# Batch 1 of a two-stage kernel: maxima and exponentials ahead of small sums, sums of the next batch at another place, left sums for two pairs in one instruction

## The chip, the cores and the metric

The kernel runs on one core of a Trainium2 chip. The metric is the device time of one execution in microseconds (us). The engines named below are TensorE (PE, with its weight loads as PEld), VectorE (DVE), ScalarE (ACT) and SyncE (SP), which issues the DMA transfers. Each engine works through its own list of instructions in order; they meet only where one waits for what another has written or read.

## The reference

An attention between tokens `x` and a small state, both ways, then a feed-forward block with the quick gelu. All is fp32. Cut to what matters:

```python
B, H, S, Ns, D = (8, 8, 512, 32, 64)      # d_model 512, d_ff 2048

scores = scale * x @ state^T               # softmax over the 32 states
xread = softmax(scores) @ state            # (B, H, 512, 64)
scores2 = scale * state @ x^T              # softmax over the 512 tokens
sread = softmax(scores2) @ x               # (B, H, 32, 64)
t = concatenate([xread, sread], axis=2)    # to (B*544, 512) for the next block
h = t @ w_in                               # (.., 2048)
g = h * (1.0 / (1.0 + np.exp(-1.702 * h)))
return g @ w_out                           # (.., 512)
```

## The kernel before

The kernel writes both products of the feed-forward block by a Strassen-Winograd scheme: 7 products of half the size instead of 8, at the price of sums of the matrices. For `w_out`, cut into quarters `B11`, `B12`, `B21`, `B22`, these are T1 to T4. For the second ("down") product most of the seven are split once more in the same way, so that each of B11, B21, B22, T1 to T4 has three small sums of its own (`low_sums`), and a third one in place (`low_third`). They are made once and kept in DRAM (`low_keep`, `low_away`), and loaded again for each batch.

```python
def low_sums(t, rooms):
    b11, b12, b21, b22 = halves_of(t)
    t1, t2, t4 = rooms
    return [(T_of, v) for v in ((t1, b12, b11), (t2, b22, t1), (t4, b21, t2))]   # DVE, L1281

def low_made(k, t, i):                 # sums made in the on-chip room low_a or low_b, and kept
    ...
def low_away(k, t):                    # sums made in a room of the tag "xT", and kept in DRAM
    room = apool.tile([P, NPR, S], FP32, tag="xT", name=f"away_{k}")...
```

The tag "xT" has one buffer. The exponentials of the scores over the tokens, `e2`, go into it too, and leave it by four DMAs (`squares<-e`):

```python
def att_s_exp(b, room=None):
    if room is None:
        room = e2_room[b] = apool.tile([P, NPR, S], FP32, tag="xT", name=f"e2_{b}")
    ...
        nc.scalar.activation(out=out, in_=src, func=AF.Exp, bias=a["mx2"][g], scale=scale, accum_out=sm)   # ACT, L386
```

A product of the small kind is seven groups of matmuls into three banks x, y, z (cut):

```python
def strassen_low(left, right, bank, R, at):
    product(x, a11, b11, True); nc.scalar.copy(y, x)      # L701
    at(1)
    product(z, s1, t1, True);   nc.scalar.copy(c22, z)    # L704
    at(2)
    product(y, s2, t2);         nc.scalar.copy(c12, y)    # L707
    at(3)
    product(x, a12, b21);       nc.scalar.copy(c11, x)    # L710
    at(4)
    product(y, a21, t3);        add(c22, y, c22)          # DVE, L697
    at(5)
    product(z, s4, b22);        add(c12, z, c12)          # DVE, L697
    at(6)
    product(y, a22, t4);        nc.scalar.copy(c21, y)    # L719
    at(7)
```

`at(i)` runs what is hooked at the place `P5.i`, `P6.i` and so on. Batch 1's down product has the order P1 (whole), P2 (whole; its halves have the hooks `P2a`, `P2b`), then P5, P6, P3, P7, P4 as small ones. In between stands the attention of batch 2: at `P2a` its scores, their transposes (`att_blocks`) and maxima (`att_s_max`), at `P2b` the exponentials.

```python
# P2, batch 1
product(bank(1), A_of(0, 1), B21, "P2")
tt(osb, bank(1), k1)               # DVE, L748: frees the bank that P5's second small product uses
```

The down product of batch 0 is done in eight pairs of blocks instead, because `w_out` is still arriving and being rounded at that time. Each pair `i` has four sums of the left matrix and four of the right one, on DVE, as instructions of 128 x 256:

```python
def pair_sums(i):
    ...
    steps = [
        (s1, a21, a22, ALU.add), (T1[:, f], B12[:, f], B11[:, f]), (s2, s1, a11), (t2, B22[:, f], T1[:, f]),
        (a21, a11, a21), (t4, B21[:, f], t2), (s4, a12, s2), (B12[:, f], B22[:, f], B12[:, f]),
    ]
    for v in steps if i else steps[::2] + steps[1::2]:
        tt(*v)                     # L1308
```

## Time and profile before

| | before |
|---|---|
| time, median of three runs | 703.92 us (703.5 to 704.36) |
| span of the profiled execution | 699.9 us |
| granted TensorE clock | 1.00 |
| PE idle from 160 to 175 us (15 us) | 2.89 us |
| PE idle from 175 to 187 us | 0.39 us |
| PE idle from 187 to 203 us | 0.00 us |
| PE idle from 203 to 230 us | 1.14 us |
| DVE busy from 187 to 203 us (16 us) | 15.86 us |

The rows of a stretch come from the table of busy time by stretches: its length less what the engine was busy. In it, 145 to 203 us is the down product of batch 1 with the attention of batch 2 beside it, and 203 to 230 us is batch 2's up product and the beginning of its down product. A releaser (the `<-`) is what ended an engine's wait. "PEld" is the weight load ahead of a matmul; it runs beside the matmul before.

### The profile page before, as it was taken

The page shows a single profiled execution, that of the slowest core. Times are in us where ns is not written, and L with a number is a line of the kernel's source. Part 1 is how long each engine was busy: PE and PEld are TensorE (multiplying, and loading weights), DVE is VectorE, ACT ScalarE, POOL GpSimd, SP SyncE. Part 2 cuts the span into 40 slices and gives each one's busy share as a digit, 9 for nine tenths or more (in the row PEclk, how much of TensorE's full clock was granted, in tenths as well). Part 3 has the DMA queues.
Part 4 walks back from the last instruction along what each step waited for, and adds up shares of the span by engine and source line. Part 5 has one row for each costly group of instructions (what it writes and reads, how often), then busy time and mean ns, then how long its engine had stood idle before and what let it go on. Part 6 is the DMA issues. An engine that isn't in the chain of part 4 may idle for free.

```text
span 699.9 us, 13779 instructions
## 1 busy us (share of the span) xinstructions
PE 683.3 (98%) x5357; PEld 578.5 (83%) x5359; DVE 571.7 (82%) x1226; ACT 320.7 (46%) x704; POOL 0.8 (0%) x8
## 2 busy tenths in 40 slices
PE   8989999998999999999999999999999999999996
PEld 3433587776898799889988999889988998999995
DVE  6999998998869989697969886988778895887540
ACT  5688843223336523654355434653376236422420
POOL 0000000000000000000000000000000000000000
PEclk9999999999999999999999999999999999999999
DMA  8921337056423474436551674157433740251001
GB/s 233 364 75 58 122 121 178 7 195 203 158 73 86 150 242 138 80 84 214 156 110 31 178 219 115 21 138 234 139 54 106 239 140 16 73 153 52 11 2 30
DMA packets 106321, 87.41 MB, mean 125 GB/s; under 512 B 64784, under 2 KB 85776, under 8 KB 106256
## 3 DMA queue, kind: packets, MB, share of 16 engines
q1 hardware_dynamic: 106256, 86.53, 42.5%
q8 instruction: 43, 0.70, 0.4%
q14 instruction: 22, 0.18, 0.1%
HBM read 68.94 MB, written 17.56 MB: 124 GB/s over the span
## 4 chain that ended last, share of the span: by engine, by line
PE 88%; DVE 5%; ACT 4%; DMA 2%; issue 1%; SPq 0%; DVEq 0%; ACTq 0%
PE low L692 27%; PE o L692 14%; PE o L1111 13%; PE upx L1111 5%; PE h L547 4%; PE o L1354 4%; PE M L329 4%; PE down L1354 3%; PE o L589 2%; PE upw L1111 2%; PE down_up L547 2%; PE o L741 1%; PE o L329 1%; PE warm L127 1%; PE upx_sr L1111 1%; DMA out_dram<-osb_sr 1%
## 5 line engine op out<-in xcount | busy, mean ns | idle before, releaser
L692 PE MATMUL low<-w_out,g 128*128 128x128 f32 x416 | 54.3, 276 | 0.0
L692 PEld LDWEIGHTS low<-w_out,g 128*128 128x128 f32 x416 | 50.5, 192 | 4.5 <-issue 3.4
L1111 PE MATMUL o<-ta,M 128*128 128x256 f32 x192 | 49.9, 382 | 0.0
L1111 PE MATMUL upx<-aT,M 128*128 128x256 f32 x192 | 49.3, 379 | 0.0
L692 PE MATMUL low<-low,g 128*128 128x128 f32 x336 | 43.5, 276 | 0.4 <-DVE later L697 0.4
L692 PEld LDWEIGHTS low<-low,g 128*128 128x128 f32 x336 | 40.3, 192 | 0.7 <-DVE later L697 0.6
L1111 PEld LDWEIGHTS o<-ta,M 128*128 128x128 f32 x192 | 35.5, 190 | 6.0 <-ACT g L1157 1.6
L1111 PEld LDWEIGHTS upx<-aT,M 128*128 128x128 f32 x192 | 36.0, 190 | 4.7
L476 ACT COPY M<-M 128x512 f32<-128x512 f32 x59 | 30.7, 594 | 16.9 <-PE M L329 16.9
L1117 ACT ACTIVATE g<-o 128x512 f32<-128x512 f32 (+1 forms) x56 | 31.4, 560 | 10.2 <-PE o L1111 10.2
L692 PE MATMUL low<-sums,later 128*128 128x128 f32 x280 | 35.8, 275 | 0.0
L692 PEld LDWEIGHTS low<-sums,later 128*128 128x128 f32 x280 | 33.6, 192 | 0.1
L329 PE MATMUL M<-w_in,stT 64*32 64x512 f32 x472 | 32.3, 595 | 0.4 <-ACT sr L524 0.4
L1111 PE MATMUL o<-ta,ms 128*128 128x256 f32 x120 | 30.8, 379 | 0.0
L547 PE MATMUL h<-aT,M 128*128 128x512 f32 x64 | 28.7, 599 | 1.4 <-ACT M L476 1.4
L1117 ACT ACTIVATE g<-g 128x512 f32<-128x512 f32 (+1 forms) x28 | 16.8, 600 | 23.4 <-DVE g L1120 23.4
L547 PEld LDWEIGHTS h<-aT,M 128*128 128x128 f32 x64 | 11.8, 190 | 18.3 <-issue 12.0
L1157 ACT COPY g<-o 128x512 f32<-128x512 f32 (+1 forms) x28 | 15.5, 555 | 24.4 <-PE o L1111 24.4
L227 ACT ACTIVATE low<-low,edge 128x512 f32<-128x512 int32 x30 | 21.5, 717 | 9.3 <-DVE low L216 9.2
L1111 PEld LDWEIGHTS o<-ta,ms 128*128 128x128 f32 x120 | 22.8, 190 | 3.1
L1111 PE MATMUL o<-aT,m 128*128 128x256 f32 x96 | 24.6, 379 | 0.0
L692 PEld LDWEIGHTS o<-w_out,g 128*128 128x128 f32 x160 | 19.4, 192 | 5.0 <-issue 5.0
(290 smaller groups left out, 1650.8 us busy)
## 6 DMA issues: line engine op xcount, KB each, us to landing
low<-low SPq DMA_DIRECT2D x108, 256.0 KB, 3.4
low<-low SPq DMA_DIRECT2D x11, 768.0 KB, 4.4
later<-in_moe_w_out_dram SPq DMA_DIRECT2D x16, 512.0 KB, 3.5
w_out<-in_moe_w_in_dram SPq DMA_DIRECT2D x12, 512.0 KB, 5.6
xsq<-in_x_dram SPq DMA_DIRECT2D x96, 64.0 KB, 2.4
xn<-in_x_dram SPq DMA_DIRECT2D x12, 512.0 KB, 4.5
out_dram<-osb SPq DMA_DIRECT2D x15, 256.0 KB, 2.2
out_dram<-later SPq DMA_DIRECT2D x14, 256.0 KB, 2.1
```

Of the source, the lines that this page charges most:

```text
L127: nc.tensor.matmul(ps, zeros[:, :P], zeros, start=True, stop=True)
L227: nc.scalar.activation(out=sc.bitcast(FP32), in_=sc, func=AF.Relu, bias=edge[0], scale=-8.0)
L329: nc.tensor.matmul(ps[g][st], A[b]["stT"][rows, st], rhs(rows, j), start=True, stop=True)
L476: nc.scalar.copy(m[:, g], ps[g])
L547: nc.tensor.matmul(hps, lhs[i], rhs[i], start=(i == 0), stop=(i == n - 1))
L589: nc.tensor.matmul(ps[:, r], lhs[f][:, P * r : P * (r + 1)], rhs[:, f], start=(first and r == 0 and f == 0), stop=(f == HF - 1), skip_grou ...
L692: nc.tensor.matmul(ps, lhs[f], rhs[:, f], start=(first and f == 0), stop=(f == QF - 1), skip_group_check=True)
L741: nc.tensor.matmul(ps[:, r], lhs[f][:, P * r : P * (r + 1)], rhs[:, f], start=(r == 0 and f == 0), stop=(f == HF - 1), skip_group_check=True,)
L1111: nc.tensor.matmul(ps[:, k], lhs[i][:, o : o + P], rhs[i], start=(first and k == 0 and i == 0), stop=(i == n - 1), skip_group_check=True,)
L1117: nc.scalar.activation(out=dst, in_=src, func=AF.Gelu_apprx_sigmoid)
L1157: nc.scalar.copy(c12, Y(u))
L1354: nc.tensor.matmul(ps7[name][:, HN * r : HN * (r + 1)], lhs[:, P * r : P * (r + 1)], rhs, start=(i == 0 and r == 0), stop=(i == HF - 1), s ...
```

## The change

Four things are moved; no matmul is added or taken away, and DVE has 16 instructions less.

- Pairs of batch 0: the left sums of two pairs are made in one instruction each (128 x 512 in place of twice 128 x 256), in rooms with four places; in the first pair the transposes of the exponentials stand between products P1 and P2, and batch 1's exponentials are made and scaled ahead of batch 0's.
- Batch 1, P2: T4's sums leave the place ahead of the maxima; the exponentials come at `P2a`, directly behind the maxima, ahead of T2's sums. T4's sums are made in P5 and P6, and the third sums of T3 and T4 a little later than before.
- B11's sums, which stood in batch 2's up product, are made ahead of it; B21's, which were spread over it and over the first small product, are made at once at its first free place.
- For this the helpers `left_sums`, `turns_of`, `T4_sum` and the rooms `s_rooms` are new.

It is meant to let the instructions that others wait for come ahead of the sums that nobody waits for yet.

```diff
-        at(p3, att_s_exp, b)
+        at("P2a" if first else p3, att_s_exp, b)
...
         if b == 2:
-            m0, m1 = (low_sums(t, r) for t, r in ((B11, low_b), (B21, low_a)))
             t0, t1, t2, t3 = ((turn_x, (b + 1, i)) for i in range(NPR))
-            more = [
-                [*m0, (low_keep, (0, turn_rooms[1]))],
-                [(low_third, (B11,)), t0],
-                [t1, t2, m1[0]],
-                [t3, m1[1]],
-            ]
-            for i, v in enumerate(more):
+            for i, v in enumerate([[], [t0], [t1, t2], [t3]]):
...
-    att_s_exp(0, room[:, :NG])
-    att_s_exp(1, room[:, NG:])
+    for b in (1, 0):
+        att_s_exp(b, room[:, NG * b : NG * (b + 1)])
     rounds(3)
-    att_s_norm(0)
-    att_s_norm(1)
+    for b in (1, 0):
+        att_s_norm(b)
...
+    def left_sums(i):
+
+        u = ORDER[i] // 2
+        (a11, a21), (a12, a22) = quarters(0, u, S), quarters(0, HF // 2 + u, S)
+        s1, s2, s4 = (v[:, i % 4 : i % 4 + 2] for v in s_rooms)
+        return [(tt, v) for v in ((s1, a21, a22, ALU.add), (s2, s1, a11), (a21, a11, a21), (s4, a12, s2))]
...
+        left = left_sums(i) if i % 2 == 0 else []
+        if i == 0:
+            first = left[:3]
+            turns_of(first)
+            turns_of(steps[:1] + left[3:] + steps[1:])
+        else:
+            turns_of([v for k in range(4) for v in left[k : k + 1] + steps[k : k + 1]])
...
         if i == 0:
-            pair(i, "P1", "P2")
+            pair(i, "P1")
             for b in (1, 0):
                 for g in range(NG):
                     att_eT(b, g, b == 1)
+            pair(i, "P2")
...
+    def T4_sum(i):
+
+        if i == 0:
+            away4.append(away(4))
+        fn, args = low_sums(T4, low_parts(away4[0]))[i]
+        fn(*args)
+        if i == 2:
+            low_keep(4, away4[0])
+
     for b in range(1, B):
+        if b == 2:
+
+            turns_of(low_sums(B11, low_b))
+            low_keep(0, turn_rooms[1])
+            low_third(B11)
         if b > 1:
-            ahead = {"P1.1": [(up_strassen(b, S, *parts_x(b), A[b]["sums"]), ())]}
-            if b == 2:
-                ahead["P1.5"] = [low_sums(B21, low_a)[2], (low_keep, (1, turn_rooms[0]))]
-                ahead["P1.6"] = [(low_third, (B21,))]
+            beside = [(turns_of, ([*low_sums(B21, low_a), (low_keep, (1, turn_rooms[0])), (low_third, (B21,))],))]
+            ahead = {"P1.1": [(up_strassen(b, S, *parts_x(b), A[b]["sums"], beside if b == 2 else ()), ())]}
         else:
             ahead = {
-                "P2a": [(low_away, (4, T4))],
                 "P2b": [(low_made, (2, T2, 0)), (low_third, (T2,))],
+                "P5.4": [(T4_sum, (0,))],
+                "P5.6": [(T4_sum, (1,))],
+                "P6.2": [(T4_sum, (2,))],
                 "P6.4": [(low_third, (B22,))],
-                "P3.1": [(low_third, (T3,))],
-                "P3.2": [(low_third, (T4,))],
+                "P3.4": [(low_third, (T3,))],
+                "P7.3": [(low_third, (T4,))],
             }
```

## The prediction

> **What bounds the kernel now.** I read four views, from coarse to fine. The first is the first part of the page, to see which engine fills the span.

> ```profile
> span 699.9 us, 13779 instructions
> ...
> PE 683.3 (98%) x5357; PEld 578.5 (83%) x5359; DVE 571.7 (82%) x1226; ACT 320.7 (46%) x704; POOL 0.8 (0%) x8
> ```

> TensorE (PE) is busy for 683.3 of 699.9 us. The change neither adds nor removes a matmul, so its whole possible gain is inside the 16.6 us in which PE stood still, and most of those lie in the start and the end that it doesn't touch. The second view, who waited for whom with PE alone, names the still time that it can touch (columns: waiting group, releaser, us in total, times, longest).

> ```profile
> PE o L692 <- DVE osb L748: 2.0, 1, 2.0
> ...
> PE low L692 <- DVE spare_M L748: 1.1, 1, 1.1
> ...
> PE low L692 <- ACT low L701: 0.9, 1, 0.9
> ...
> PE M L329 <- ACT sr L524: 0.4, 1, 0.4
> PE low L692 <- DVE later L697: 0.4, 1, 0.4
> PE o L1354 <- ACT sums L550: 0.3, 1, 0.3
> ```

> Together 5.1 us. The third view, the instructions in order of time from 145 to 174 us, shows what is behind the first and third of these (columns: start, us, engine, line, operation, idle time before).

> ```profile
> 160.15 2.05 ACT L476 COPY M<-M 128x512 f32<-128x512 f32 x4 [4.80 <-PE M L329]
> 160.85 3.32 PEld L741 LDWEIGHTS o<-w_out,g 128*128 128x128 f32 x16 [0.84 <-issue]
> ...
> 161.28 1.31 DVE L360 STREAM_TRANSPOSE e<-o 128x512 f32<-128x512 f32 x2
> 161.38 0.34 SPq L652 DMA_DIRECT2D low<-away  x1
> ...
> 165.80 1.28 ACT L386 ACT_TABLE_LOAD   x1 [3.59 <-DMA low<-away]
> ...
> 166.70 0.68 DVE L748 TENSOR_TENSOR osb<-o,g 128x512 f32<-128x512 f32 x1
> ...
> 167.44 1.16 PE L692 MATMUL o<-low,spare_M 128*128 128x128 f32 x8 [1.98 <-DVE osb L748]
> ...
> 169.13 0.33 ACT L701 COPY low<-low 128x128 f32<-128x128 f32 x1
> ...
> 169.32 2.71 SPq L484 DMA_DIRECT2D squares<-e  x4
> ...
> 169.51 1.16 PE L692 MATMUL low<-low,spare_M 128*128 128x128 f32 x8 [0.92 <-ACT low L701]
> ```

> There are two chains. VectorE (DVE) makes T4's sums from 159.15 to 161.28, then transposes and maxima, then T2's sums, and only at 166.70 the addition `osb` that frees a bank: PE stands still for 1.98 us. ScalarE (ACT) is done with its copies at 162.2, but the exponentials go into the buffer that T4's sums used, and wait 3.59 us until those have left it by DMA; the small copy L701 stands behind them: 0.92 us. The fourth view, the same from 196 to 240 us, shows the third wait, the 1.1 us in batch 2's first product: a sum of B21 stands directly ahead of the sum PE needs.

> ```profile
> 228.34 0.65 DVE L1281 TENSOR_TENSOR low<-w_out,low 128x512 f32<-128x512 f32 x1
> 228.91 0.75 DVE L748 TENSOR_TENSOR spare_M<-g,g 128x256 f32<-128x256 f32 x2
> ...
> 229.47 1.13 PE L692 MATMUL low<-low,spare_M 128*128 128x128 f32 x8 [1.15 <-DVE spare_M L748]
> ```

> [...]I count only idle time with a named releaser. [...]the trace shows 1.28 us and the exponential directly behind it (165.80 to 167.09), so I charge 1.28. [...](256 KB to the output land in 2.1 to 2.2 us).

> **Part 1, pairs.** Left sums for two pairs at once: 32 instructions of 256 become 16 of 512. In the trace a 256 starts about 0.34 us after the last, a 512 0.60: 2 x 0.34 - 0.60 = 0.08, times 16 = 1.3 us of DVE. But from 91 to 145 us PE is busy 54.00 of 54.00, so I count nothing. Ahead of it, the transposes eT now come before product P2. Both need the same gelu (it frees the first transpose's bank), so P2 cannot start before 79.2 and neither can the transposes; what moves is the four copies of eT on ACT, from 80.83 to the end of the gelus at 80.63: **0.2 us**, passed on through the wait of M L329.

> **Part 2, batch 1's maxima and exponentials ahead of T2 and T4.** DVE starts the transposes of the scores when the scores are done, about 159.25, not 161.28. Up to `osb` it then has the same work as before, 166.70 - 161.28 = 5.42 us, so `osb` starts at 164.67 and ends at 165.35. The product that waits for it could start, by the matmuls alone, about 165.3; weight load included I take 165.4, against 167.44. On ACT: copies end 162.2, table load to 163.5, the exponentials (2.2 us, 167.09 to 169.29) to 165.65, L701 to 165.95; the third product starts at 166.3, not 169.51. So far 3.2 us gained.

> **Part 3, where T4's sums went.** They now stand behind the fourth and sixth small product of P5 and the second of P6, in the same buffer as the exponentials. The first must therefore wait until the exponentials have left by the four DMAs squares<-e. These can be issued at 165.7; four issues took 2.71 us, so until 168.4, and then the last must land: 2.2 us after it was issued at 167.7 (the output's 2.1 to 2.2) is 169.9, and the queue is busy with x and with T2's sums until then, so I estimate 170.5. DVE reaches that sum at 164.67 + 7 operations of 0.60 = 168.9, and stands until 170.5, then 0.6 for the sum. Directly behind it is the addition L697 that the seventh product of P5 waits for; PE would come to that product at 169.9. Addition until 171.4: **PE stands about 1.4 us where it did not before.** From 3.2 that leaves 1.8.

> Further on T4's remaining two sums (0.6 each) fit in 1.57 and 1.50 us in which DVE waited for PE before. The third sums of T3 and T4 leave the stretch around 182.8 and 184.7: the addition L697 that PE waited for 0.39 us (186.24) is then early: gain 2.2. T4's third comes back in P7, where DVE is busy 15.86 of 16.00 us (187 to 203) and has no room: give back about 0.5. **Part 2 and 3: 1.7 us.**

> **Part 4, B11 and B21.** B11's four operations (2.65 us) now stand ahead of batch 2's up products, where DVE waited 3.14 us for ACT: free. B21's four follow the first addition and push the next by 0.4 us, which has slack. At the end the sum at 228.34 is gone; DVE's chain behind the addition at 224.59 (five operations, about 3.7 us) still ends at 228.3, so the wait of 1.15 shrinks by **0.6 us**, not wholly.

> **Sum:** 0.2 + 1.7 + 0.6 = 2.5 us; 703.92 - 2.5 = 701.4 us.

> **Rivals.** (a) The DMA is early: all waits go. If squares<-e has landed by 168.9, part 3's stall is nil and DVE keeps its lead: 3.2 + 0.4 + 0.6 + 0.2 = 4.4, so about 699.5. For it: without T4's 768 KB the queue has less ahead of these DMAs. Against: issue and landing alone reach 169.9. (b) A new wait takes the place of the old. The DMA lands at 172 or later, the stall is 3 us, and DVE, with no slack from 187 to 203, carries the loss on: gain 0 to 0.8, about 703.5. For it: before, the queue moved nothing much until about 1.7 us after the first issue (169.32 to 171). (c) DVE is the bound of batch 1's second product: what leaves one place on DVE only comes back in another, as it does the same work but for 1.3 us. Its idle time from 160 to 187 is 27 - 23.4 = 3.6 us, which is enough for a gain of some 2 but not of 4: about 702. (d) Nothing in the pairs: if the first pair's double-width sums delay product P6 there, 0.3 us is lost; T2's sum for it is done about when it was before (85.5), so I give this little.

> **Range and chances.** Rivals (a) and (b) span 699.5 to 703.5; the runs before spread by 0.9 us. Range 699.4 to 703.3. 2% is 14 us, nearly three times all the waits concerned: within 2% 0.985, faster 0.01, slower 0.005.

> **What would show it.** Right: DVE's `osb` starts directly after T2's sums and no wait for it over 0.2 us is left on PE; the table load follows the copies near 162.2; DVE waits 1 to 2 us for the DMA squares<-e ahead of the first T4 sum, and PE as long, less its lead, for L697; the wait at batch 2's first product is about 0.5. Wrong: no wait of DVE for squares<-e (rival a), or one above 2.5 us (b); or PE waits in P7 and P4 that sum to over 1 us (c); or any loss in 91 to 145 us.

## The result and the profile after

| | before | after |
|---|---|---|
| time, median | 704.01 us (703.5 to 704.36, 4 runs) | 700.44 us (699.63 to 701.43, 4 runs) |
| ratio, 95% interval | | 0.9951 (0.9933 to 0.9968) |
| span of the profiled execution | 699.9 us | 699.1 us |

The change gains 3.57 us, within 2%; 701.4 had been predicted. The profiled execution shows only 0.8 us of it, and that is the first riddle. The first part of the page of after:

```profile
span 699.1 us, 13774 instructions
...
PE 684.5 (98%) x5359; PEld 579.6 (83%) x5359; DVE 571.5 (82%) x1210; ACT 321.0 (46%) x704; POOL 0.8 (0%) x8
```

DVE has its 16 instructions less (1210 for 1226) and the same busy time. PE does the same matmuls and is busy 1.2 us longer: some of them were slower (the record of a small matmul takes 421 ns at 174 us, 275 at 178). Who waited for whom, PE alone, in after:

```profile
PE low L692 <- DVE spare_M L697: 1.9, 1, 1.9
...
PE o L692 <- DVE osb L748: 0.6, 1, 0.6
PE eT L504 <- ACT sums L550: 0.3, 1, 0.3
...
PE low L692 <- DVE later L697: 0.2, 1, 0.2
```

Of the six waits before, 5.1 us together, those for `osb` (2.0), the exponentials' L701 (0.9), batch 2's `spare_M` (1.1) and `sr` (0.4) are gone or down to 0.6; one new wait of 1.9 has come. The sum is 3.0, so 2.1 us less. The instructions of after in order of time show how (start, us, engine, line, operation, idle time before):

```profile
159.35 1.31 DVE L360 STREAM_TRANSPOSE e<-o 128x512 f32<-128x512 f32 x2 [0.64 <-PE o L329]
...
162.13 1.28 ACT L386 ACT_TABLE_LOAD   x1
...
163.27 1.42 DVE L1274 TENSOR_TENSOR low<-sums,low 128x512 f32<-128x512 f32 x2 [0.46 <-DVE low L1274]
...
165.21 0.68 DVE L748 TENSOR_TENSOR osb<-o,g 128x512 f32<-128x512 f32 x1
...
165.64 2.75 SPq L484 DMA_DIRECT2D squares<-e  x4
...
165.95 1.16 PE L692 MATMUL o<-low,spare_M 128*128 128x128 f32 x8 [0.59 <-DVE osb L748]
...
166.95 1.06 PE L692 MATMUL low<-low,spare_M 128*128 128x128 f32 x8
...
171.64 0.69 DVE L1274 TENSOR_TENSOR away<-sums 128x512 f32<-128x512 f32 x1 [2.14 <-DMA squares<-e]
172.25 0.28 DVE L697 TENSOR_TENSOR spare_M<-low,spare_M 128x128 f32<-128x128 f32 x1
...
172.59 1.70 PE L692 MATMUL low<-low,later 128*128 128x128 f32 x8 [1.91 <-DVE spare_M L697]
```

The first half is the gain: the table load follows the copies at 162.13 (165.80 before), and P5's second and third small products start at 165.95 and 166.95, before at 167.44 and 169.51: 2.56 us earlier at the third. The second half gives most of it back. T4's first sum (171.64) stands for the four DMAs out of the buffer that it shares with the exponentials; the short addition L697 is behind it in DVE's list, and PE's seventh product behind that. P5's seventh product is only 0.60 us earlier than before (172.59 against 173.19).

And then even that is lost. The table of busy time by stretches of after, cut where the clock changes (start:end, length, busy time of PE, PEld, DVE, ACT and POOL, granted clock PEclk, DMA share, GB/s):

```profile
169.62:173.03 3.41, 1.50 (x14) 1.31 (x13) 1.39 (x3) 0.00 (x0) 0.00 (x0) 1.00 0.89 252
173.03:176.44 3.41, 3.41 (x19) 3.41 (x18) 3.34 (x12) 0.52 (x2) 0.00 (x0) 0.50 0.30 83
176.44:179.86 3.42, 3.42 (x32) 3.42 (x32) 1.66 (x3) 1.33 (x4) 0.00 (x0) 1.00 1.01 350
```

From 173.0 to 176.4, one stretch of 3.41 us that begins 0.4 us behind the end of the new wait, the clock was at 0.50; the profiled execution of before had 1.00 in all of 160 to 230 us. In that stretch it is 1.71 us from the start of eight small matmuls to the next eight (174.08 to 175.79), at 1.00 behind it 0.89 (177.00 to 177.89). From the clock of 0.50 I estimate that 3.41 us of matmuls did the work of 1.71. So the product sread of the attention (L518, `sr`), before at 187.33, comes at 187.87, 0.54 us late. Up to batch 2's first product 0.42 more are lost, in P7, where T4's third sum now stands. What is left of the gain comes in that first product:

```profile
227.36 1.05 PE L692 MATMUL low<-w_out,g 128*128 128x128 f32 x8
...
228.55 0.72 DVE L748 TENSOR_TENSOR spare_M<-g,g 128x256 f32<-128x256 f32 x2
...
229.12 1.09 PE L692 MATMUL low<-low,spare_M 128*128 128x128 f32 x8
```

It begins 0.96 us later than before (226.40), but its second small product comes 1.76 us after the first, without a wait, where it was 3.07: it starts 0.35 us earlier than before (229.47). The next landmark, the scores of batch 3's attention, is at 234.71 for 235.10: 0.39 us earlier, and with the 1.71 that the half clock cost by that estimate 2.1, which is the sum by which the waits are shorter.

### The profile page after: what moved, and what is told of

It reads as the page before. It is cut to its first block, busy times and chain, and to the rows that moved or that the text cites. A ratio compares the mean times of both kernels' runs of the same rounds, so it can differ in the third digit from the quotient of the medians.

```text
span 699.1 us, 13774 instructions
## 1 busy us (share of the span) xinstructions
PE 684.5 (98%) x5359; PEld 579.6 (83%) x5359; DVE 571.5 (82%) x1210; ACT 321.0 (46%) x704; POOL 0.8 (0%) x8
## 4 chain that ended last, share of the span: by engine, by line
PE 90%; ACT 4%; DVE 2%; DMA 2%; SPq 1%; issue 0%; DVEq 0%
PE low L692 26%; PE o L1104 15%; PE o L692 14%; PE upx L1104 6%; PE h L547 4%; PE o L1371 4%; PE M L329 4%; PE down L1371 3%; PE o L589 2%; PE upw L1104 2%; PE down_up L547 2%; PE o L741 1%; PE o L329 1%; PE warm L127 1%; PE upx_sr L1104 1%; PE sr L518 1%
## 5 line engine op out<-in xcount | busy, mean ns | idle before, releaser
L692 PE MATMUL low<-w_out,g 128*128 128x128 f32 x416 | 54.3, 276 | 0.0
L692 PEld LDWEIGHTS low<-w_out,g 128*128 128x128 f32 x416 | 50.5, 192 | 4.5 <-issue 4.2
L692 PE MATMUL low<-low,g 128*128 128x128 f32 x336 | 43.7, 277 | 0.2 <-DVE later L697 0.2
L692 PEld LDWEIGHTS low<-low,g 128*128 128x128 f32 x336 | 40.7, 194 | 0.3 <-DVE later L697 0.3
L476 ACT COPY M<-M 128x512 f32<-128x512 f32 x59 | 30.7, 595 | 16.9 <-PE M L329 16.9
L692 PE MATMUL low<-sums,later 128*128 128x128 f32 x280 | 36.7, 279 | 0.0
L692 PEld LDWEIGHTS low<-sums,later 128*128 128x128 f32 x280 | 34.4, 196 | 0.1
L329 PE MATMUL M<-w_in,stT 64*32 64x512 f32 x472 | 32.6, 595 | 0.0
L692 PE MATMUL low<-low,later 128*128 128x128 f32 x168 | 22.5, 281 | 1.9 <-DVE spare_M L697 1.9
```

Of the source, the lines that this page charges most:

```text
L329: nc.tensor.matmul(ps[g][st], A[b]["stT"][rows, st], rhs(rows, j), start=True, stop=True)
L476: nc.scalar.copy(m[:, g], ps[g])
L692: nc.tensor.matmul(ps, lhs[f], rhs[:, f], start=(first and f == 0), stop=(f == QF - 1), skip_group_check=True)
```

## The experiments

Two theories stood for the measured 3.57 us. In the expectations, W says that waits make the time: each version is faster by what its named waits are shorter, part by part. C says that a good part is the granted clock: PE standing still for some 2 us can bring a stretch of half clock, in some executions and not in others, and the change makes that rarer. "The theory of the prediction" is W with the sizes of the prediction, and rival c is the one named there (DVE as the bound).

Each execution records its mean granted clock. One stretch as above takes 0.0024 from it (half of 3.41 in some 700 us), the slow clock at the kernel's end some more: it lasts 0.14 us in the profile of before and 0.43 in that of after, and I estimate some 2 to 3.5 us for e5's, if all of its loss lies there (a mean of 0.998, and 1.00 in every 4 us up to 368). So a mean of 0.998 or more is read as "no such stretch" and one below as "one or more"; for a single run at the edge that reading is uncertain. Before stood at 703.77 us (52 runs) beside the first four kernels and 703.48 (22 runs) beside the last four.

**e1: the moves in batch 1 alone.** On the kernel before:

```diff
-        at(p3, att_s_exp, b)
+        at("P2a" if first else p3, att_s_exp, b)
...
-                "P2a": [(low_away, (4, T4))],
+                "P5.4": [(T4_sum, (0,))],
+                "P5.6": [(T4_sum, (1,))],
+                "P6.2": [(T4_sum, (2,))],
...
-                "P3.1": [(low_third, (T3,))],
-                "P3.2": [(low_third, (T4,))],
+                "P3.4": [(low_third, (T3,))],
+                "P7.3": [(low_third, (T4,))],
```

> The kernel before with the second and third part of the change alone: T4's sums leave the place ahead of the maxima and stand in P5 and P6, behind the exponentials' buffer; pairs and B11/B21 as before. By the waits alone (theory W): PE's waits of 1.98 and 0.92 us behind P5's first products shrink to 0.6 us, the new wait ahead of P5's seventh product is 1.9 us, so about 0.4 to 1 us faster than before. If the granted clock has a part (theory C: PE's standing still for some 2 us within P5 lets the clock fall to half for about 3 us afterwards, in most runs of the kernel before too), the runs spread by 1.5 us or more with the clock's mean, and the median is 0 to 3 us below before.

Measured: 700.77 us (700.11 to 701.46, 7 runs), ratio 0.9958 (0.9942 to 0.9973); mean clock 0.998 or more in all seven. Its DVE in order of time:

```profile
165.05 0.68 DVE L748 TENSOR_TENSOR osb<-o,g 128x512 f32<-128x512 f32 x1
...
170.89 0.69 DVE L1281 TENSOR_TENSOR away<-sums 128x512 f32<-128x512 f32 x1 [1.55 <-DMA squares<-e]
171.50 0.28 DVE L697 TENSOR_TENSOR spare_M<-low,spare_M 128x128 f32<-128x128 f32 x1
```

The same new wait, 1.3 us on PE here. By its waits this part is worth 1.6 us (5.1 to 3.5); by the medians 3.0. The other 1.4 go with the clock: a mean below 0.998 in no run of e1, in 44 of 52 of before. W's 0.4 to 1 us was too little, and the spread that C expected, 1.5 us or more, was 1.35.

**e2: the sums of B11 and B21 alone.** On the kernel before:

```diff
-            m0, m1 = (low_sums(t, r) for t, r in ((B11, low_b), (B21, low_a)))
...
+        if b == 2:
+            turns_of(low_sums(B11, low_b))
+            low_keep(0, turn_rooms[1])
+            low_third(B11)
...
+            beside = [(turns_of, ([*low_sums(B21, low_a), (low_keep, (1, turn_rooms[0])), (low_third, (B21,))],))]
```

> The kernel before with the fourth part alone: B11's sums ahead of batch 2's up product, B21's at its first free place. Both theories: only PE's wait of 1.15 us in batch 2's first small product goes (the profile after shows none over 0.2 us there): 0.8 to 1.2 us faster. I had predicted 0.6.

Measured: 702.95 us (700.12 to 704.57, 22 runs), ratio 0.9982 (0.9972 to 0.9992). The waits for `osb` (1.9) and L701 (0.9) stay, and a mean clock below 0.998 with them, in 20 of 22 runs. The wait at batch 2 is gone wholly. Instructions in order of time, of before and then of e2:

```profile
222.92 0.63 ACT L1117 ACTIVATE g<-g 128x512 f32<-128x512 f32 x1 [1.77 <-DVE g L1120]
...
223.93 0.57 ACT L1157 COPY g<-o 128x512 f32<-128x512 f32 x1
...
224.59 0.69 DVE L1120 TENSOR_TENSOR o<-upw,g 128x512 f32<-128x512 f32 x1
```

```profile
221.99 0.63 ACT L1110 ACTIVATE g<-g 128x512 f32<-128x512 f32 x1 [0.76 <-DVE g L1113]
...
223.29 0.59 ACT L1150 COPY g<-o 128x512 f32<-128x512 f32 x1 [0.18 <-PE o L1104]
...
223.91 0.70 DVE L1113 TENSOR_TENSOR o<-upw,g 128x512 f32<-128x512 f32 x1 [0.74 <-ACT g L1150]
...
227.68 0.72 DVE L748 TENSOR_TENSOR spare_M<-g,g 128x256 f32<-128x256 f32 x2
...
228.24 1.10 PE L692 MATMUL low<-low,spare_M 128*128 128x128 f32 x8
```

Without the small sums between its others, DVE hands ACT the gelu's input 0.93 us earlier (222.92, 221.99), ACT's copy comes 0.64 earlier, and DVE's chain to `spare_M` starts 0.68 earlier (224.59, 223.91). From the first small product to the second it is 1.75 us, 3.07 before: 1.32 gained.

**e3: the pairs alone** (left sums for two pairs in one instruction, the transposes ahead of P2, batch 1 ahead of batch 0, as in the diff of the change; batches 1 and later as before).

> The kernel before with the first part alone: left sums for two pairs at once, batch 1's exponentials first, the transposes of the exponentials between P1 and P2 of the first pair. Both theories: 0.1 to 0.2 us faster; PE busy 54.0 of 54.0 us from 91 to 145 us.

Measured: 701.70 us (700.65 to 705.34, 22 runs), ratio 0.9975 (0.9964 to 0.9985); 16 of 22 runs at a mean clock of 0.998 or more. Both theories had expected 0.1 to 0.2 us; it is 2.1 by all runs, more than e2. DVE of e3:

```profile
158.09 0.68 DVE L1281 TENSOR_TENSOR away<-sums 128x512 f32<-128x512 f32 x1
...
165.64 0.68 DVE L748 TENSOR_TENSOR osb<-o,g 128x512 f32<-128x512 f32 x1
```

The same instructions are at 159.15 and 166.70 in before: 1.06 us, and PE's wait there:

```profile
PE o L692 <- DVE osb L748: 1.0, 1, 1.0
```

1.0 in place of 2.0. But DVE's saved time doesn't simply ride along to that place. In between DVE stands for blocks of `w_out`, in before and then in e3:

```profile
118.64 0.94 SPq L194 DMA_DIRECT2D later<-in_moe_w_out_dram  x2
122.38 0.43 DVE L216 TENSOR_SCALAR low<-later 128x512 int32<-128x512 int32 x1 [2.25 <-DMA later<-in_moe_w_out_dram]
```

```profile
117.74 0.93 SPq L194 DMA_DIRECT2D later<-in_moe_w_out_dram  x2
121.27 0.43 DVE L216 TENSOR_SCALAR low<-later 128x512 int32<-128x512 int32 x1 [1.90 <-DMA later<-in_moe_w_out_dram]
```

DVE comes to this wait 0.76 us earlier (119.37, 120.13 in before), and that alone would only make it longer. What passes the lead on is the issue: in before the queue waits for DVE's pair sums (L1308, 0.4 us) ahead of this transfer, so with fewer of them it is issued 0.90 us earlier, and DVE goes on 1.11 us earlier. From there to `osb` DVE stands only 0.3 us more, in both. How much of it arrives depends on when the transfer lands: in the six profiles with the pairs (e3, after, e6 to e9) it is issued at 117.74 to 117.90 and DVE goes on at 121.27 to 122.37, in the four without at 118.54 to 118.87 and 122.38 to 122.53. e3's profile has the earliest landing of all, so its 1.06 us is the most of six. The wait of L701 is still 0.9, as expected of a part that doesn't touch ACT there.

**e5: before, with PE kept busy in the two waits.** In the kernel before, matmuls of the identity with itself into an unused bank, 12 ahead of P5's second small product and 5 ahead of the third, in batch 1 only; they add work that leads to nothing:

```diff
+            turn[0] += 1
+            n = warm.get(turn[0], 0)          # {2: 12, 3: 5}
+            if n:
+                spare = att_ps([P, FC], f"warm_{turn[0]}")
+                for _ in range(n):
+                    nc.tensor.matmul(spare[:, :P], ident, ident, start=True, stop=True)
```

> The kernel before, all its waits left as they are, with 12 dummy matmuls of 128x128 (the identity with itself, into a free bank that nobody reads) ahead of P5's second small product and 5 ahead of the third: they fill 1.3 of 1.98 and 0.55 of 0.92 us in which PE stood still, and delay nothing. Theory W (the waits alone): the time of before, 703.9 us, within 0.3. Theory C (the clock falls after PE has stood still): the granted clock stays 1.00 in all runs and the median is about 701.7 us, that of the profiled run of before, whose clock was 1.000; spread below 0.6 us.

Measured: 703.14 us (702.61 to 704.31, 14 runs), ratio 0.9994 (0.9983 to 1.0005): the time is the same. The mean clock is 0.998 or more in all 14 runs, in before in 8 of 52. PE of e5:

```profile
165.18 2.84 PE L698 MATMUL warm<-ident 128*128 128x128 f32 x24
167.86 1.06 PE L700 MATMUL o<-low,spare_M 128*128 128x128 f32 x8
168.76 1.28 PE L698 MATMUL warm<-ident 128*128 128x128 f32 x10
```

I made them too long: a matmul of fp32 is two records here and takes 0.24 us (2.84 by 12), and the wait was 1.98. So the two small products came at 167.86 and 169.87, each about 0.4 us later than in before (167.44 and 169.51). Both theories missed the time: W had 703.9 within 0.3, C 701.7 with a spread below 0.6 (it is 1.7). What was gained by the clock went to that delay in part, so the run doesn't measure what the clock alone is worth; with the 0.4 us put back, an estimate is 1.0 us (703.77 - 703.14 + 0.4). What the run does show is that the still time brings the low means: with PE busy in those two waits no run has one, and the spread is half (standard deviation 0.54 us against 1.06).

**e6: the change again,** unaltered, for more runs.

> The changed kernel as it is, once more beside the others, for its granted clock in many runs. Theory C (PE's standing still in P5 lets the clock fall to half for 3.4 us in some runs): runs with a mean clock of 0.998 or more near 699.7 us, runs of 0.997 about 1.2 us higher; fewer of the latter than the 44 of 52 that the kernel before had. Theory W (the waits alone): no relation of time and clock; median 700.4.

Measured: 699.98 us (699.24 to 701.97, 16 runs), ratio 0.9957 (0.9946 to 0.9968). 14 runs at a mean clock of 0.998 or more have a median of 699.92, the two others 701.59 and 701.97. One run at 0.999 took 701.36, so the mean doesn't explain every slow run. In the runs of before beside it, 9 of 22 are at 0.998 or more, with a median of 702.25. So 702.25 - 699.92 = 2.3 us of the 3.5 (703.48 - 699.98) are there without any fall of the clock, which goes with the 2.1 us by which the named waits are shorter; the other 1.2 go with the fall being rarer. The profiled executions of after happen to be ones with the fall, here too (one stretch of about 3.4 us at half clock, about 173.8 to 177.2, worked out from mean clocks of 0.96 in 160 to 175 us and 0.91 in 175 to 187): hence the 0.8 us of its span.

**e7: the change, with T4's sums two places later,** so that none stands ahead of L697 before the seventh product:

```diff
-                "P5.4": [(T4_sum, (0,))],
-                "P5.6": [(T4_sum, (1,))],
+                "P5.6": [(T4_sum, (0,))],
+                "P6.1": [(T4_sum, (1,))],
                 "P6.2": [(T4_sum, (2,))],
```

> The changed kernel with T4's three sums later: behind the sixth small product of P5 and the first and second of P6, and so behind the addition that P5's seventh product waits for. If the wait for the exponentials' DMA ahead of the first T4 sum is what holds PE (theory of the prediction): PE's wait of 1.91 us for L697 goes, the first T4 sum waits for squares<-e at most 0.8 us and nobody waits for it, and the clock stays 1.00: 698.0 us, 1.5 to 2.5 below the changed kernel. If DVE's work as a whole is the bound from 160 to 203 us (rival c): the wait turns up again in P6, P3, P7 or P4, and the time is that of the changed kernel within 0.5.

Measured: 697.74 us (697.58 to 698.38, 6 runs), ratio 0.9926 (0.9909 to 0.9943), all at 0.998 or more. PE's waits in e7, and then its instructions in order of time:

```profile
PE o L692 <- DVE osb L748: 0.6, 1, 0.6
PE eT L504 <- ACT sums L550: 0.3, 1, 0.3
...
PE low L692 <- DVE later L697: 0.2, 1, 0.2
```

```profile
165.60 2.82 SPq L484 DMA_DIRECT2D squares<-e  x4
...
169.86 0.29 DVE L697 TENSOR_TENSOR spare_M<-low,spare_M 128x128 f32<-128x128 f32 x1 [0.39 <-PE low L692]
...
170.48 1.06 PE L692 MATMUL low<-low,later 128*128 128x128 f32 x8
...
171.56 0.69 DVE L1274 TENSOR_TENSOR away<-sums 128x512 f32<-128x512 f32 x1
```

L697 comes at 169.86 and not 172.25, the seventh product at 170.48 and not 172.59: 2.11 us earlier. T4's first sum starts at 171.56, as before this edit (171.64), but now DVE has work until then and nobody stands behind it. The new wait was worth 2.2 us (699.92 to 697.74); 1.9 is what the profile shows as its length.

**e8: the same, all three in P6** (`P6.1`, `P6.2`, `P6.3`).

> The changed kernel with T4's sums behind the first, second and third small product of P6. Theory of the prediction: as the run before, with no wait of DVE for the DMA at all: 698.0 us, within 0.5 of the run before. Rival c (DVE is the bound): later sums crowd P6 and P3, PE waits there by 0.5 us or more, and it is slower than the run before.

Measured: 697.90 us (697.18 to 698.56, 6 runs), ratio 0.9925 (0.9905 to 0.9944). Like e7. DVE is busy 25.78 of the 27 us from 160 to 187, and PE still doesn't wait for it there beyond e7's.

**e9: the change, with PE kept busy in its two waits** (the edit of e5 with `{2: 2, 7: 7}`).

> The changed kernel with dummy matmuls of 128x128 (the identity with itself, into a free bank that nobody reads) in PE's waits within P5: 2 (about 0.45 us) ahead of the second small product and 7 (about 1.56 us) ahead of the seventh. No wait is taken away. Theory C: the clock does not fall in any run (mean 0.998 or more), and the median is that of the changed kernel's undisturbed runs, 699.7, plus up to 0.3 that the dummies cost; spread below 1 us. Theory W: the same distribution as the changed kernel, 699.6 to 701.4.

Measured: 700.29 us (699.86 to 700.89, 7 runs), ratio 0.9958 (0.9942 to 0.9975); all seven at 0.998 or more. It is no faster than the runs of the change without the fall (699.92): seven dummies cover the wait but don't shorten it (the seventh product starts at 172.66, in after at 172.59). That none of the seven has the fall says little: of the change's own 20 runs only four had a low mean.

**What the runs say together.** Named waits of PE (the six of before and their successors) against medians of runs at a mean clock of 0.998 or more:

| kernel | waits, us | less than before | median of such runs | less than before |
|---|---|---|---|---|
| before | 5.1 | | 702.55 (8) and 702.25 (9) | |
| e3, pairs | 3.9 | 1.2 | 701.59 (16) | 1.0 |
| e1, batch 1 | 3.5 | 1.6 | 700.77 (7) | 1.8 |
| after | 3.0 | 2.1 | 699.92 (14) | 2.3 |
| e7 | 1.1 | 4.0 | 697.74 (6) | 4.5 |

e1 and e3 are held against 702.55, after and e7 against 702.25. (e2 is left out: only two of its runs are of this kind. Their median is 700.39, 2.2 less, for waits that are 1.2 less.) W holds for these runs within half a us. What is beyond goes with the clock, as C has it: the whole change has 3.5 us by all runs. The parts don't add up: 3.0 (e1), 0.8 (e2) and 2.1 (e3) by all runs are 5.9, for two reasons. e1 and e3 end the same wait for `osb`, and each alone already takes most of the falls of the clock away (a mean below 0.998 in none of 7 and in 6 of 22 runs, in before in 44 of 52).

## Why the prediction was right, point by point

The time was right (701.4, measured 700.44), and so was the mechanism: one wait goes, another takes its place by way of a shared buffer, and batch 2's wait goes. That the number came within 1 us is in part luck: errors that cancel, and a gain by the clock that nobody had counted. Of the signs it gave, the table load near 162.2 came as stated; a wait for `osb` of at most 0.2 us, DVE's 1 to 2 us for squares<-e and the 0.5 left at batch 2 came as 0.59, 2.14 and none.

- Part 1, pairs. Right that 91 to 145 us gives nothing (PE busy 54.00 of 54.00, again) and that the transposes gain little (0.1 us at P6 of the first pair, 86.62 to 86.52, for 0.2). Wrong in "so I count nothing" of DVE's 1.3 us: that PE is full in a stretch says what DVE's time is worth there, not later. In e3's profile `osb` came 1.06 us earlier, by way of a transfer that was issued 0.90 us earlier. In the whole change nothing of it is left at `osb`, though: with T4's sums away DVE stands 0.64 us for the scores (159.35) anyway, and `osb` is at 165.05 in e1, without the pairs, and at 165.21 with them.
- Part 2. The chain is as predicted. Right for ACT: copies, table load at 162.13, exponentials, L701 at 165.47, no wait for it left. `osb` starts at 165.21, not 164.67: 0.46 of that is a gap on DVE ahead of T2's second sum that no row explains (0.46 or 0.47 in the profiles of after and e6 to e9, 0.10 in e1). So P5's second and third product are at 165.95 and 166.95 for 165.4 and 166.3, and a wait of 0.59 remains where under 0.2 was foretold.
- Part 3. Right that T4's first sum waits for squares<-e and holds up L697. DVE reaches it at 169.5 and stands 2.14 us; the transfer is there at 171.6 (170.9 in e1), not at the estimated 170.5; PE stands 1.91 and not 1.4. Gained up to there: 0.6 us, not 1.8. "L697 (186.24) is then early" was right, and worth 0.59 by the starts of the products around it (184.80 to 187.33 in before, 185.93 to 187.87 in after). The 0.5 given back in P7 was nearly right too: only 0.16 shows as a wait (15.84 busy of 16.00), but by the starts it loses 0.43 (194.92 to 196.70 in before, 195.45 to 197.66 in after).
- Part 4. The wait goes wholly: 1.3 us (e2: 3.07 to 1.75), not 0.6. The term that was too small is the start of DVE's chain: I left the addition at 224.59, but its input from ACT had itself been late because of DVE's small sums.
- Not foreseen: the granted clock. By the runs, some 1.2 of the 3.5 us. The whole possible gain was sought in the 16.6 us in which PE stood still; at half clock PE counts as busy (3.41 of 3.41 us from 173.03 in after), so such a loss is not among them, and the profile of before had none.
- Rival a (early DMA, 699.5) fails on 2.14 us of waiting; rival b (DMA at 172 or later) was nearly true by its landing, 171.6, but DVE doesn't carry the loss on: e7, without the stall, loses as much in P7 (191.78 to 193.99). Rival c falls by e7 and e8: 4.5 us of gain where it allowed 2. Rival d isn't seen.

In the sum: 0.2 + 1.7 + 0.6 stood for about 0.1 + 0.7 + 1.3 of waits (the middle one: at the seventh product 0.60, of which 0.1 came from the pairs, 0.59 where L697 was waited for, less 0.43 in P7) and 1.2 of clock.

## What to carry to other kernels

A sum that is taken off a chain must not go behind a buffer whose transfer is still out and ahead of a short instruction that PE needs: two places later it cost nothing, and that version (e7, 697.74 us) beats both kernels. Time saved on an engine where nobody waits for it can still be worth something later, when it moves the issue of a transfer for which the engine itself stands next (e3: issued 0.90 us earlier at 118, `osb` 1.06 us earlier at 166); how much arrives varies with the landing. When waits of some 2 us come or go (1.98 in before, 1.91 in after), look at the granted clock stretch by stretch and at every run's mean, not at one profile alone.

## What was not expected of the hardware

```profile
163.85:167.26 3.41, 1.61 (x12) 1.34 (x10) 3.31 (x7) 1.45 (x2) 0.00 (x0) 1.00 0.98 307
167.26:170.67 3.41, 2.32 (x18) 2.13 (x19) 3.41 (x7) 2.40 (x6) 0.00 (x0) 1.00 0.75 290
```

1.80 and 1.09 us stood still, and no fall. Where the waits lie in the grid is thus a likely reason, not a proven one, why the same waits bring the fall in one execution and not in the next. That the still time within one stretch of the grid counts is my assumption. On it, I estimate from the traces how much of P5's waits one stretch of 3.41 us can hold at most: 2.3 us in before (3.41 less the 1.15 of matmuls between its two waits), 1.9 in after, 1.8 in e3, 1.3 in e1, 0.6 in e7 and e8, 0.4 or less in e5 and e9. Mean clocks below 0.998 are where the estimate is large: 44 of 52 and 13 of 22 runs of before, 20 of 22 of e2 (which keeps before's waits), 4 of 20 of after (2 of 4, and 2 of 16 in e6), 6 of 22 of e3, and none of e1, e5, e7, e8 and e9 (40 runs together). That is argued from few profiles: none of before or e2 has the fall itself, where between 1.3 us (e1) and 1.8 (e3) the falls begin isn't shown, and a stretch at the very end of before (692.91 to 696.33), with 1.98 us still, brought none. The runs with low means are longer by 1.5 us (704.04 to 702.55) to 2.3 (704.58 to 702.25). Not settled either is what DVE's gap of 0.46 us is.

The last of the four transfers squares<-e is issued around 167.7 (165.64 plus three quarters of 2.75) and there at 171.6, when DVE's wait for it ends: 3.9 us (3.0 in e1, 167.9 to 170.9). The prediction took 2.2 us, from transfers of 256 KB to the output; in after, where the DMA engines were busy for 0.96 of the time from 167.70 to 171.64 us (219 GB/s), it was nearly twice that.
